# Attention and mixture of experts in one kernel: the first expert's weight casts ahead of the exponentials, six of their eight low parts on GpSimd

## The chip, the cores and the metric

The kernel runs on one core of a Trainium2 chip. The metric is the device time of one execution in microseconds; for the kernel before it is 588.51 us, the median of three runs (588.12 to 589.81).

## What is computed

```
attention, for 8 batches x 8 heads, 576 rows of 64:
    k_p, v_p = means of 8 neighbouring rows of k, v           # 72 rows each
    attn = softmax(q @ k_p.T / 8) @ v_p
x = attn as 4608 tokens of 512
experts, for each token:
    expert = argmax(x @ w_gate);  gate = softmax(x @ w_gate)[expert]
    out = gate * (relu(x @ w1[expert]) @ w2[expert])          # 512 -> 1024 -> 512, 8 experts
```

All tensors are float32. The expert products are made from a rounded part and a rest: a weight W is held as a "high part" (the weight rounded by a cast to the type fp32r) and a "low part" (the weight minus its high part), and a product is the sum of three matmuls.

## The kernel before, in words

The first 170 us or so of the 587.5 us span are attention. It runs as one hand-written loop over 36 tiles `t` of 128 tokens, in four groups `g` of nine. What a pass of the loop emits goes to each engine's queue in that order, and each engine takes its queue strictly in order. Per pass `t`, the steps are:

- `p_transpose(t)`: TensorE turns the exponentials `P` into `pP` (L314), ScalarE copies them to `pt` (L315, two copies).
- `scores(t+2)`: TensorE writes the scores into the one buffer `pS` (L288); VectorE takes their maximum `mx` (L294) and subtracts it into `sd` (L299). `sd` frees `pS` for the next pass's scores.
- `q_transpose(t+3)`: TensorE, then a ScalarE copy to `qT` (L280). In some passes there follow `v_expand` (L232, copy `V` L234: passes 25 to 28) or `kv_transpose` with four small copies (L212, L214: passes 20, 22 and 23).
- `weights(t+2)`: ScalarE's exponential of `sd` into `P` (L307); after it, in every third pass, a small exponential `ex` for the router (L382).
- `weigh(t)`: TensorE, `pt` times `V` into the one buffer `pU` (L330). A pass is counted below from one start of `weigh` to the next.
- `scale(t)`: VectorE divides (`r` L342, `lh` L344, `xe` L346); `xe` frees `pU`. Small steps of the router are woven in on VectorE: `rg`, `rm`, `rd`, `rk` at the end of each pass with `t % 3 == 2` (L412 to L416), `rn` and `ro` one pass later between `mx` and `sd` (L417, L377), then a count on TensorE and `rp`, `carry`, `rs` (L394, L395, L421). GpSimd multiplies `rp` by `ro` (L426), copies the token numbers (L422), casts a row index `ix` (L406) and issues the scatter of a tile's rows to DRAM (L449); VectorE makes the index as `rf` (L401, or L427 for the last batches).
- `w_split`: the last step of the passes 21 and 24 to 30. One eighth of the first expert's weights, loaded three passes earlier into one of four buffers (`w_load`, L460 on SyncE's queue), is cast on ScalarE (L466) and its low part is made by a subtraction (L467) with two inputs in SBUF, on VectorE, but on GpSimd in the passes 26 and 29.

"Cast 25" and "low part 25" mean those of pass 25 below, and `sd` 27 the `sd` of tile 27, which pass 25 makes. After the loop the tail of attention multiplies the first products with these weights, a plan is made, and the expert stage fills the rest of the span.

Of the kernel before, what the change touches and what calls it, by code (L numbers as in the profile page):

```python
# [15 lines left out]
ALU = mybir.AluOpType  # L16
# [17 lines left out]
NB = 3  # L34
# [6 lines left out]
W0T = (21, *range(24, 31))  # L41
# [12 lines left out]
def f32(a):  # L54
    return a.bitcast(F32)
# [48 lines left out]
def attention(ctx, outer, tc, q, k, v, wg, w1v, w2v, xs, W, cst, carry, tab, banks):  # L104
    nc = tc.nc
# [75 lines left out]
    def kv_load(g, i):  # L181


        src, c0 = (v if i % 2 else k), 3 * (i // 2)

        raw = u0["XE"][:, 0:3, :] if (g, i) == (0, 1) else kraw.tile([P, 3, 512], F32, tag="raw", name=f"raw{g}_{i}")
        sv = src[2 * g : 2 * g + 2].rearrange("b h (k8 x) d -> (b h k8) (x d)", k8=8)
        nc.sync.dma_start(out=raw, in_=sv[:, c0 * 512 : c0 * 512 + 1536].rearrange("p (c f) -> p c f", c=3))
        raws[g, i] = raw

    def kv_pool(g, i, eng):

        raw, c0, o = raws.pop((g, i)), 3 * (i // 2), 64 * (i % 2)

        def add(n):
            out = kvp[:, c0 : c0 + 3, o : o + 64] if n == 64 else raw[:, :, 0:n]
            return lambda: eng.tensor_tensor(out=out, in0=raw[:, :, 0:n], in1=raw[:, :, n : 2 * n], op=ALU.add)  # L197

        return [add(n) for n in (256, 128, 64)]
# [27 lines left out]
    def v_expand(g, i, bank, take=nc.scalar.copy):  # L227

        b, a = i // 2, i % 2
        for c in range(3 * a, 3 * a + 3):  # L230
            o, m, j = CH[c][0], CH[c][3], BL[c]
            nc.tensor.matmul(bank[0:R, j * 72 : (j + m) * 72], lhsT=vT[:, b * H * KP + o : b * H * KP + o + R],  # L232
                             rhs=wrhs[:, a, j : j + m].rearrange("p j f -> p (j f)"), start=True, stop=True)
        take(out=Vs[g % 2][0:R, b, a, :, 0 : D + NE], in_=bank[0:R, 0:360].rearrange("p (j f) -> p j f", f=D + NE))  # L234
# [9 lines left out]
    def q_load(g, b):  # L244
        t = e2.tile([P, 4, H, D], F32, tag="qa", name=f"qa{g}_{b}")
        src = q[2 * g + b, :, 0:512, :]
        if 2 * g + b < COPIED:

            t = t.rearrange("p x h d -> p (x h d)").rearrange("p (h x) -> p h x", h=H)
            nc.sync.dma_start(out=t, in_=src.rearrange("h (p x) d -> p h (x d)", x=4))  # L250
        else:
            for x in range(4):
                nc.sync.dma_start(out=t[:, x], in_=src.rearrange("h (p x) d -> x p h d", x=4)[x])
        qa[g, b] = t

    def qm_load(g):
        m = e1.tile([P, H, D], F32, tag="qm", name=f"qm{g}")
        for j in range(2):
            nc.sync.dma_start(out=m[64 * j : 64 * j + 64], in_=q[2 * g + j, :, 512:576, :].rearrange("h p d -> p h d"))
        qa[g, 2] = m  # L260
# [14 lines left out]
    def q_transpose(t):  # L275
        src = qr.pop(t).rearrange("p h d -> p (h d)")
        for j in range(4):
            nc.tensor.transpose(pq[:, j * P : (j + 1) * P], src[:, j * P : (j + 1) * P], ident)  # L278
        qT[t] = p3.tile([P, 512], F32, tag="qT", name=f"qT{t}")
        nc.scalar.copy(out=qT[t], in_=pq)  # L280

    def scores(t):
        g = t // NT
        for j in range(4):
            for p0, b in [(0, 0), (64, 1)] if KIND(t) == 4 else [(0, parts(t)[0][2]), (64, parts(t)[0][2])]:
                for hp in range(2):
                    r = slice(64 * hp, 64 * hp + 64)
                    nc.tensor.matmul(pS[p0 : p0 + 64, hp, j * SK : (j + 1) * SK], lhsT=qT[t][r, j * P + p0 : j * P + p0 + 64],  # L288
                                     rhs=kTs[g % 2][r, b, j, hp * SK : (hp + 1) * SK], start=True, stop=True, skip_group_check=True)
        for count, _ in counts:  # L290
            count()
        s4 = pS[:, :, 0:288].rearrange("p a (h x) -> p a h x", h=4)
        mx = p2.tile([P, 2, 4], F32, tag="mx", name=f"mx{t}")
        nc.vector.tensor_reduce(out=mx, in_=s4, axis=AX.X, op=ALU.max)  # L294
        if t - 2 in stores:
            stores.pop(t - 2)()
        weave()
        sd = p2.tile([P, 2, 4, SK], F32, tag="sd", name=f"sd{t}")
        nc.vector.tensor_tensor(out=sd, in0=s4, in1=mx.unsqueeze(3).to_broadcast([P, 2, 4, SK]), op=ALU.subtract)  # L299
        run(counted for _, counted in counts)  # L300
        counts.clear()
        weave(1, True)
        sds[t] = sd
# [5 lines left out]
    def p_transpose(t, take=nc.scalar.copy):  # L309
        pt[t] = [p2.tile([P, 3 * P], F32, tag=f"pt{a}", name=f"pt{a}_{t}") for a in range(2)]  # L310
        for a in range(2):
            for c in range(3):
                o = CH[3 * a + c][0]
                nc.tensor.transpose(pPs[a][0:R, c * P : (c + 1) * P], Ps[t % 2][:, o : o + R], ident)  # L314
            take(out=pt[t][a][0:R], in_=pPs[a][0:R, 0 : 3 * P])  # L315
# [141 lines left out]
    def w_load(i):  # L457

        raw = kraw.tile([P, 1024], F32, tag="raw", name=f"w0_{i}")
        nc.sync.dma_start(out=raw.rearrange("p (c f) -> p c f", c=4 if i < 4 else 2), in_=load_piece(w1v, w2v, 0, i))  # L460
        w0[i] = raw

    def w_split(i):
        raw = w0.pop(i)
        c, a = slice((i % 4) * 1024, (i % 4 + 1) * 1024), 0 if i < 4 else 2
        nc.scalar.copy(out=W[:, a, c], in_=raw)  # L466
        (nc.gpsimd if W0T[i] % NB == 2 else nc.vector).tensor_tensor(out=W[:, a + 1, c], in0=raw, in1=f32(W[:, a, c]), op=ALU.subtract)  # L467

# [44 lines left out]
    def run(fs):  # L515
        for f in fs:
            f()
# [67 lines left out]
    for t in range(total):  # L585
        g, i = divmod(t, NT)
        more = g + 1 < NG
        for (G, at), j in loads.items():
            if at == t:
                kv_load(G, j)  # L590
        if more:
            if i == 2:
                q_load(g + 1, 0)
            if i == 4:
                qm_load(g + 1)
            if i == 6:
                q_load(g + 1, 1)
        if t in first:
            run(kv_pool(*first.pop(t), nc.gpsimd))
        for at, n, *gj in adds:  # L600
            if at == t:
                third = tuple(gj)
                if third not in pieces:
                    pieces[third] = kv_pool(*gj, vec)
                halves.extend(pieces[third][:n])
                del pieces[third][:n]
        if t + 3 in W0T:
            w_load(W0T.index(t + 3))
        if 0 < t < total - 2:
            p_transpose(t)  # L610
        if 2 < t + 2 < total:
            scores(t + 2)
        counts.extend(picked)
        picked.clear()
        if t - 1 in pools:
            run(kv_pool(*pools.pop(t - 1), nc.gpsimd))
        if t + 3 < total:
            q_transpose(t + 3)
        elif t == total - 3:
            for s in (1, 2):  # L620
                x_split(s)()
        at = (2, 4, 5) if g else (3, 5, 6)
        if more and i in at:
            kv_transpose(g + 1, at.index(i), pm)
        if more and i >= 7:
            v_expand(g + 1, i - 7, pm)
        if i < 2:
            v_expand(g, 2 + i, pm)
        if t + 4 < total:
            q_copy(t + 4)  # L630
        if t + 2 < total:
            weights(t + 2)
        run(powers)
        powers.clear()
        if t == total - 3:
            p_transpose(t + 1)
        weigh(t)
        if t == total - 3:
            x_low = x_split(3)
            p_transpose(t + 2)  # L640
        if t == total - 4:
            x_split(0)()
        if t == total - 1:
            multiply(4)
        if t >= total - 3:
            weave(7)
        held = steps[:] if t == total - 1 else []
        if held:
            steps.clear()
        scale(t)  # L650
        if t == total - 3:
            x_low()
        for bt, (t0, nb) in enumerate(batches):
            if t == t0 + nb - 1:
                route(bt)
        if t in W0T:
            w_split(W0T.index(t))
        if 20 <= t < 24:
            clear_rows(t - 20)
        if t == total - 7:  # L660
            x_load()
        if t == total - 5:
            x_open()
            begun_load()
# [1107 lines left out]
```

## Time and profile before

| | |
|---|---|
| median of 3 runs | 588.51 us |
| profiled execution, its own time | 589.0 us |
| its span | 587.5 us |
| TensorE busy | 560.3 us (95%) |
| VectorE busy | 373.9 us (64%) |
| ScalarE busy | 244.8 us (42%) |
| GpSimd busy | 196.7 us (33%) |
[...]

The table's shares are averages over attention and experts. In the passes with a weight piece the picture is another: there TensorE stands still for part of each pass, and VectorE is the engine with the most work.

### The profile page before, as it was taken

To read this page: it belongs to the slowest core of one execution; us is meant where nothing else is said; L and a number is where in the kernel's file an instruction comes from. 1 tells how busy PE (TensorE), PEld (TensorE's weight loads), DVE (VectorE), ACT (ScalarE), POOL (GpSimd) and SP (SyncE) were. 2 spreads that over 40 slices of the span, in tenths; PEclk is the share of its full clock that TensorE was granted. 3 is DMA by queue.
4 is the path that set the end of the run, shared out by engine and by line. 5 is a ranking of instruction groups with operands and counts; after the bars stand their busy time and mean duration, and the time that the engine had idled before them with its cause. 6 is when DMAs were issued, how large, how long until landed. Compare 5 with 4: busy or idle time off the path is not lost.

```text
span 587.5 us, 13579 instructions
## 1 busy us (share of the span) xinstructions
PE 560.3 (95%) x4334; PEld 499.3 (85%) x4334; DVE 373.9 (64%) x749; ACT 244.8 (42%) x451; POOL 196.7 (33%) x293
## 2 busy tenths in 40 slices
PE   6899999998898999999999999999999999999994
PEld 5788989897787888879988889888899888888994
DVE  6699999988884224657949671685428956143221
ACT  2677676776631102357545420434115842021110
POOL 7456765625432042126232222151113451101101
PEclk9999999999999999999999999999999999999999
DMA  8969999994422647446996852046412750101001
GB/s 313 367 222 291 312 297 286 264 261 148 141 90 76 185 146 249 123 152 189 256 316 188 245 175 63 20 134 196 133 56 70 226 161 23 57 0 40 37 4 56
DMA packets 89013, 96.50 MB, mean 164 GB/s; under 512 B 38174, under 2 KB 69918, under 8 KB 88864
## 3 DMA queue, kind: packets, MB, share of 16 engines
q1 hardware_dynamic: 79472, 74.22, 43.3%
q0 software_dynamic: 8848, 20.55, 9.7%
q8 instruction: 60, 0.98, 0.7%
q14 instruction: 89, 0.73, 0.4%
q10 hardware_dynamic: 544, 0.02, 0.1%
HBM read 72.68 MB, written 26.00 MB: 168 GB/s over the span
## 4 chain that ended last, share of the span: by engine, by line
PE 76%; DVE 14%; issue 3%; DMA 3%; ACT 2%; POOLq 1%; DVEq 1%; SPq 0%; POOL 0%; ACTq 0%
PE pU L964 31%; PE pP L907 20%; PE pq L907 10%; PE pU L330 4%; DVE sd L299 2%; DVE mx L294 2%; PE pS L288 2%; DMA XE<-in_v_dram 2%; PE pP L314 2%; PE pP L506 2%; PE pq L278 1%; DVE xe L346 1%; DVE raw L197 1%; PE pm L232 1%; DVE W L467 1%
## 5 line engine op out<-in xcount | busy, mean ns | idle before, releaser
L964 PE MATMUL pU<-W,H 128*128 128x512 f32 x912 | 200.4, 380 | 2.5 <-issue 1.3
L964 PEld LDWEIGHTS pU<-W,H 128*128 128x128 f32 x912 | 171.6, 189 | 28.2 <-issue 2.7
L1595 POOL DMA_INDIRECT out_dram<-Y,GT x51 | 60.4, 1184 | 195.3 <-DVE Y L1389 164.6
L907 PE MATMUL pP<-X,W 128*128 128x512 f32 (+3 forms) x660 | 121.9, 340 | 2.0 <-DVEq L1645 1.5
L907 PEld LDWEIGHTS pP<-X,W 128*128 128x128 f32 x660 | 108.6, 190 | 11.9 <-DVEq L1645 1.9
L1099 ACT ACTIVATE H<-pP 128x512 fp32r<-128x512 f32 x56 | 33.5, 598 | 141.9 <-PE pP L907 135.5
L1389 DVE TENSOR_SCALAR Y<-pU,GT 128x512 f32<-128x512 f32 x36 | 26.8, 747 | 89.8 <-PE pU L964 89.8
L1120 DVE SCALAR_TENSOR_TENSOR H<-pP,H 128x512 fp32r<-128x512 f32 (+1 forms) x62 | 39.8, 643 | 57.1 <-ACT H L1099 54.9
L1205 ACT CAST W<-ST 128x1024 fp32r<-128x1024 f32 x56 | 56.8, 1050 | 23.9 <-PE pU L964 19.6
L1213 DVE TENSOR_TENSOR W<-ST,W 128x1024 fp32r<-128x1024 f32 x54 | 64.2, 1213 | 3.8 <-ACT W L1205 3.7
L907 PE MATMUL pq<-X,W 128*128 128x512 f32 (+3 forms) x324 | 62.4, 342 | 0.9 <-issue 0.9
L330 PE MATMUL pU<-V,pt 110*128 110x146 f32 (+3 forms) x468 | 56.9, 283 | 3.0 <-ACT pt L315 1.7
L907 PEld LDWEIGHTS pq<-X,W 128*128 128x128 f32 x324 | 53.8, 190 | 6.1 <-issue 1.3
L330 PEld LDWEIGHTS pU<-V,pt 110*128 110x128 f32 (+3 forms) x468 | 51.4, 179 | 5.4 <-ACT pt L315 3.8
L1602 POOL DMA_DIRECT2D GT<-dispatched x44 | 24.4, 554 | 83.3 <-issue 82.1
L1099 ACT ACTIVATE H<-pq 128x512 fp32r<-128x512 f32 x28 | 16.7, 598 | 60.3 <-PE pq L907 60.2
L449 POOL DMA_INDIRECT dispatched<-xe,ix x36 | 36.0, 1001 | 13.5 <-POOL ix L406 11.3
L1174 DVE STREAM_TRANSPOSE pS<-XE 128x512 f32<-128x512 f32 x26 | 37.7, 1492 | 0.0
L307 ACT ACTIVATE P<-sd 128x576 f32<-128x576 f32 x36 | 24.8, 688 | 24.4 <-DVE sd L299 19.1
L1120 DVE SCALAR_TENSOR_TENSOR H<-pq,H 128x512 fp32r<-128x512 f32 (+1 forms) x30 | 19.6, 654 | 23.7 <-ACT H L1099 23.1
L315 ACT COPY pt<-pP 110x384 f32<-110x384 f32 x72 | 30.8, 479 | 4.1 <-PE pP L314 3.5
L197 POOL TENSOR_TENSOR raw<-raw 128x768 f32<-128x768 f32 (+1 forms) x18 | 27.5, 1527 | 9.6 <-DMA raw<-in_v_dram 5.4
(213 smaller groups left out, 648.9 us busy)
## 6 DMA issues: line engine op xcount, KB each, us to landing
ST<-in_moe_w_dram SPq DMA_DIRECT2D x56, 512.0 KB, 5.8
raw<-in_k_dram SPq DMA_DIRECT2D x12, 768.0 KB, 7.8
raw<-in_v_dram SPq DMA_DIRECT2D x11, 768.0 KB, 9.2
XE<-dispatched SPq DMA_DIRECT2D x104, 64.0 KB, 4.0
qa<-in_q_dram SPq DMA_DIRECT2D x24, 256.0 KB, 6.8
w<-in_moe_w_dram SPq DMA_DIRECT2D x8, 512.0 KB, 6.8
XE<-dispatched SPq DMA_DIRECT2D x15, 256.0 KB, 4.4
qa<-in_q_dram SPq DMA_DIRECT2D x2, 1024.0 KB, 11.4
```

The costliest lines, as they stand in the source:

```text
L197: return lambda: eng.tensor_tensor(out=out, in0=raw[:, :, 0:n], in1=raw[:, :, n : 2 * n], op=ALU.add)
L315: take(out=pt[t][a][0:R], in_=pPs[a][0:R, 0 : 3 * P])
L330: nc.tensor.matmul(pu[p0 : p0 + n, a, h * VW : (h + m) * VW], lhsT=pt[t][a][0:r, c % 3 * P + p0 : c % 3 * P + p0 + n], rhs=Vs[g % 2][0:r, ...
L449: apart(nc.gpsimd.indirect_dma_start(out=xs, out_offset=bass.IndirectOffsetOnAxis(ap=at, axis=0), in_=rows, in_offset=None))
L907: r = pe.matmul(out=pH[g % 3][:, :m], lhsT=w1s(w, f, k), rhs=x, start=i == 0, stop=i == len(passes) - 1)
L964: r = pe.matmul(out=pY[:, s % 2, :], lhsT=h, rhs=in_turn(w[:, k * 512 : (k + 1) * 512]), start=start and i == 0, stop=stop and i == len(ps ...
L1099: act.activation(out=HH[:, f, o], in_=src[:, o], func=AF.Relu).then_inc(Q["A_h"], 1)
L1120: return dve.scalar_tensor_tensor(out=dst[:, f, to], in0=src[:, at], scalar=0.0, in1=f32(HH[:, f, at]), op0=ALU.max, op1=ALU.subtract)
L1174: dve.transpose(out=pX[:, s % 2, :].rearrange("p (c a g t) -> p c g t a", c=4, a=2, g=4), in_=XE[u % 2][:, s, :].rearrange("p (g r c) -> p ...
L1205: act.copy(out=(W1H if i < 4 else W2H)[:, o], in_=ST[:, i, :]).then_inc(Q["A_s1" if i < 4 else "A_s2"], 1)
L1213: eng.tensor_tensor(out=(W1L if i < 4 else W2L)[:, o], in0=ST[:, i, :], in1=f32((W1H if i < 4 else W2H)[:, o]), op=ALU.subtract).then_inc( ...
L1595: pool.indirect_dma_start(out=out, out_offset=bass.IndirectOffsetOnAxis(ap=GT[:, u, s, 1:2].bitcast(I32), axis=0), in_=Y[:, s, :], in_offs ...
```

## The change

In a pass with a weight piece the cast is emitted before `q_copy` and `weights(t+2)`, so it stands ahead of the exponential in ScalarE's queue. The low part stays at the end of the pass, but the engines are exchanged: GpSimd makes those of the passes 21, 24, 25, 27, 28 and 30, VectorE those of 26 and 29.

```
         nc.scalar.copy(out=W[:, a, c], in_=raw)
-        (nc.gpsimd if W0T[i] % NB == 2 else nc.vector).tensor_tensor(out=W[:, a + 1, c], in0=raw, in1=f32(W[:, a, c]), op=ALU.subtract)
+        return lambda: (nc.vector if W0T[i] % NB == 2 else nc.gpsimd).tensor_tensor(out=W[:, a + 1, c], in0=raw, in1=f32(W[:, a, c]), op=ALU.subtract)
...
             v_expand(g, 2 + i, pm)
+        if t in W0T:
+            w_low = w_split(W0T.index(t))
         if t + 4 < total:
             q_copy(t + 4)
...
         if t in W0T:
-            w_split(W0T.index(t))
+            w_low()
```

ScalarE, pass 28, as a difference (`w_5` is this pass's weight piece, `P` and `sd` belong to tile 30, `pt_29` to the next pass):

```order
 L280 COPY qT_2395<-pq 128x512
 L234 COPY V_147<-pm 110x5x72
+L466 CAST W<-w_5_2144 128x1024
 L307 ACTIVATE P_148<-sd_2382 128x2x4x72
-L466 CAST W<-w_5_2144 128x1024
 L315 COPY pt_29_2422<-pP_65 110x384
 L315 COPY pt_29_2423<-pP_66 110x384
```

The cast has moved from between the exponential and the copies of `pt` to ahead of the exponential.

GpSimd, the passes 28 to 31, before:

```order
L406 CAST ix_2277<-rf_2276 128x1
L449 DMA dispatched<-xe_2136,ix_2277 38400x514
L467 TENSOR_TENSOR W<-w_6_2212,W 128x1024
L426 TENSOR_TENSOR rp_2473<-rp_2473,ro_2472 128x24
L422 COPY xe_2339<-tok 128x3
```

and now:

```order
L406 CAST ix_2278<-rf_2277 128x1
L449 DMA dispatched<-xe_2137,ix_2278 38400x514
L467 TENSOR_TENSOR W<-w_5_2144,W 128x1024
L467 TENSOR_TENSOR W<-w_7_2284,W 128x1024
L426 TENSOR_TENSOR rp_2474<-rp_2474,ro_2473 128x24
L422 COPY xe_2340<-tok 128x3
```

Where one low part (29) stood behind the last of three scatters, two (28 and 30) now stand back to back, with nothing between them.

VectorE, the end of pass 29 and the beginning of pass 30, now:

```order
L414 TENSOR_TENSOR rd_2471<-rg_2470,rm_2475 128x24
L416 SCALAR_TENSOR_TENSOR rk_2472<-rd_2471,order 128x24
L467 TENSOR_TENSOR W<-w_6_2212,W 128x1024
L294 TENSOR_REDUCE mx_2528<-pS 128x8
L417 TENSOR_REDUCE rn_2476<-rk_2472 128x3
L377 TENSOR_TENSOR ro_2473<-rk_2472,rn_2476 128x24
L299 TENSOR_TENSOR sd_2532<-pS,mx_2528 128x576
```

Low part 29 now stands between `rk` and `mx`; before, `mx` followed `rk` directly.

## Rows read from the trace of the kernel before

**Rows 1.** Busy us per pass (start:end, length, each engine; clock, DMA, GB/s), passes 23–31.
```profile
117.92:121.27 3.35, 3.35 (x56) 3.09 (x55) 2.48 (x9) 3.17 (x8) 1.21 (x2) 1.00 1.08 296
121.27:125.44 4.17, 4.17 (x67) 3.87 (x65) 3.23 (x11) 2.75 (x6) 1.15 (x2) 1.00 0.97 234
125.44:129.99 4.55, 4.20 (x61) 3.90 (x61) 4.11 (x12) 3.34 (x7) 1.54 (x4) 1.00 0.98 331
129.99:134.31 4.32, 4.24 (x63) 3.81 (x61) 4.18 (x12) 3.11 (x7) 1.56 (x3) 1.00 0.67 205
134.31:139.28 4.97, 4.46 (x65) 3.94 (x65) 4.01 (x9) 3.33 (x8) 3.13 (x3) 1.00 0.36 109
139.28:143.85 4.57, 3.69 (x55) 3.19 (x55) 4.19 (x15) 3.37 (x7) 1.94 (x6) 1.00 0.36 143
143.85:148.49 4.64, 3.65 (x54) 3.12 (x55) 4.47 (x11) 2.72 (x6) 3.57 (x6) 1.00 0.39 144
148.49:153.46 4.97, 3.78 (x59) 3.25 (x59) 4.01 (x8) 2.98 (x7) 2.01 (x1) 1.00 0.47 110
153.46:157.33 3.87, 3.43 (x66) 2.89 (x67) 3.73 (x12) 2.09 (x5) 0.55 (x3) 1.00 0.56 168
```
The engines stand in the order TensorE, its weight loads, VectorE, ScalarE, GpSimd.

**Rows 2.** Timeline (start us, us, engine, line; idle before), passes 25 to 26.
```profile
128.41 1.03 ACT L466 CAST W<-w 128x1024 fp32r<-128x1024 f32 x1
...
129.48 1.23 DVE L467 TENSOR_TENSOR W<-w,W 128x1024 fp32r<-128x1024 f32 x1 [0.41 <-ACT W L466]
...
130.62 0.75 DVE L294 TENSOR_REDUCE mx<-pS 128x8 f32<-128x576 f32 x1
...
131.40 0.76 DVE L299 TENSOR_TENSOR sd<-pS,mx 128x576 f32<-128x576 f32 x1
...
132.25 0.69 ACT L307 ACTIVATE P<-sd 128x576 f32<-128x576 f32 x1 [1.21 <-DVE sd L299]
```
**Rows 3.** Timeline of VectorE and GpSimd around low part 26.
```profile
133.95 0.75 DVE L294 TENSOR_REDUCE mx<-pS 128x8 f32<-128x576 f32 x1
133.96 2.35 POOL L467 TENSOR_TENSOR W<-w,W 128x1024 fp32r<-128x1024 f32 x1 [0.97 <-ACT W L466]
...
134.89 1.47 DVE L377 TENSOR_TENSOR ro<-rk,rn 128x24 bf16<-128x24 f32 x1
```
**Rows 4.** Timeline: VectorE and GpSimd, both with operands in SBUF, earlier passes.
```profile
45.00 0.98 DVE L197 TENSOR_TENSOR raw<-raw 128x768 f32<-128x768 f32 x1
45.11 0.92 POOL L422 COPY xe<-tok 128x3 int32<-128x3 int32 x1
...
58.07 2.90 POOL L197 TENSOR_TENSOR raw<-raw 128x768 f32<-128x768 f32 x2
60.06 1.73 DVE L197 TENSOR_TENSOR raw<-raw 128x768 f32<-128x768 f32 x1
```
**Rows 5.** Timeline: GpSimd and VectorE at the end of pass 21.
```profile
111.08 0.98 POOL L449 DMA_INDIRECT dispatched<-xe,ix  x1 [0.28 <-POOL ix L406]
...
112.88 0.35 DVE L197 TENSOR_TENSOR kvp<-raw 128x192 f32<-128x192 f32 x1
...
114.46 0.75 DVE L294 TENSOR_REDUCE mx<-pS 128x8 f32<-128x576 f32 x1
```
**Rows 6.** Timeline: `mx` behind pass 23's router steps; then passes 28 and 29.
```profile
121.46 0.75 DVE L294 TENSOR_REDUCE mx<-pS 128x8 f32<-128x576 f32 x1
...
140.91 0.18 POOL L406 CAST ix<-rf 128x1 int32<-128x1 f32 x1 [3.20 <-DVE rf L401]
...
143.02 0.68 DVE L346 TENSOR_TENSOR xe<-pU,r 128x512 f32<-128x512 f32 x1
...
146.65 0.98 POOL L449 DMA_INDIRECT dispatched<-xe,ix  x1 [0.28 <-POOL ix L406]
...
148.14 2.35 POOL L467 TENSOR_TENSOR W<-w,W 128x1024 fp32r<-128x1024 f32 x1 [0.51 <-ACT W L466]
```
**Rows 7.** The weight pieces' tile: their loads, from issue to landing.
```profile
DMA to landing us min/median/max: 3.9/6.8/10.0
```

More of the change, by code (lines that the diff above doesn't have):

```diff
@@ L466, in w_split @@
         nc.scalar.copy(out=W[:, a, c], in_=raw)
-        (nc.gpsimd if W0T[i] % NB == 2 else nc.vector).tensor_tensor(out=W[:, a + 1, c], in0=raw, in1=f32(W[:, a, c]), op=ALU.subtract)
+        return lambda: (nc.vector if W0T[i] % NB == 2 else nc.gpsimd).tensor_tensor(out=W[:, a + 1, c], in0=raw, in1=f32(W[:, a, c]), op=ALU.subtract)
     def clear_rows(s):
@@ L628, in attention @@
             v_expand(g, 2 + i, pm)
+        if t in W0T:
+            w_low = w_split(W0T.index(t))
         if t + 4 < total:
@@ L656, in attention @@
         if t in W0T:
-            w_split(W0T.index(t))
+            w_low()
         if 20 <= t < 24:
```

## The prediction

> **What bounds the kernel now.** I read the page first, then cut the attention loop into its passes, then followed the order of work through single passes. Over the span TensorE is nearly always busy, and a change on ScalarE, VectorE and GpSimd can win only where TensorE stands still. Pass by pass one sees where that is [rows 1]: pass 23, without a weight piece, lasts 3.35 us and TensorE is busy for all of it; pass 24, which has `v_expand` and the router's count on top, lasts 4.17, again all busy. The passes 25 to 31 last 4.55, 4.32, 4.97, 4.57, 4.64, 4.97 and 3.87, together 31.89, and TensorE is short of work by 0.1 to 1.2 in each. [...]
>
> What closes the pass there is a ring over two engines [rows 2]. The cast starts at 128.41, behind the exponential; the low part waits 0.41 for it and takes 1.23; `mx` stands behind the low part in VectorE's queue (130.62), then `sd` (131.40), and the next exponential, for which ScalarE has idled 1.21, starts at 132.25. From 128.41 to the next cast that is exponential 0.69, cast 1.03, low part 1.23, `mx` 0.75 and `sd` 0.76 less small overlaps, some 4.4 us, against 3.35 to 4.17 of TensorE's work. In two passes a second thing is seen [rows 3, 6]: low part 26 runs on GpSimd from 133.96 to 136.31, and VectorE's `ro`, 24 elements a row, takes 1.47 and ends with it; the same happens beside low part 29, from 148.14 to 150.49.
>
> **What the change takes out.** The cast moves into the 1.21 us that ScalarE idles ahead of the exponential [rows 2]. At 1.03 it fits; it costs nothing as long as `sd` isn't ready earlier than the cast ends. Where it does, ScalarE's work in a pass with `v_expand` is about 3.3 us [rows 1], below TensorE's 4.1, so ScalarE doesn't become the bound. The low part leaves VectorE in six passes (1.14 from its start to the next instruction's, 130.62 less 129.48) and comes onto it in two. With both gone from the ring, TensorE's own work is next in line.
>
> **What it adds.** GpSimd's low part takes 2.35 [rows 3, 6] and nobody needs its result before the first products after the loop. What it costs comes from the port. Two rows show that GpSimd and a VectorE instruction whose operands both lie in SBUF exclude each other [rows 4]: VectorE's addition at 60.06 takes 1.73 beside GpSimd's (0.98 at 45.00), and GpSimd's copy at 45.11, three elements, takes 0.92 until VectorE's addition is over. `mx`, which reads PSUM, keeps its 0.75 beside a low part [rows 3]. So I need only look where `kvp`, `rd`, `rk`, `ro` or a low part on VectorE meets a low part on GpSimd.
>
> *Pass 21.* Cast 21 now ends about 111.3, GpSimd is free at 112.06 when its scatter is issued, and low part 21 runs to 114.41. `kvp` (two SBUF inputs), which started at 112.88, now waits until then and ends about 114.65; `mx` follows at about 114.58 where it stood at 114.46 [rows 5]. What VectorE saves by giving up the low part it pays here: a loss of 0.12.
>
> *Passes 22 to 24.* No further change: 23 and 24 are full already. All starts below are those of before plus 0.12: `weigh` 25 at 125.56.
>
> *Passes 25 and 26.* Both have `v_expand`, without the count; I take TensorE's own 4.1 (4.17 less a little over 0.1 for the count, with an estimate of 0.05 for the remaining stalls). Gains 0.45 and 0.22. `weigh` 27 at 133.76.
>
> *Pass 27.* Before, `ro` was held for 1.47 instead of about 0.18 by low part 26 [rows 3]. That stall goes, 1.29. But low part 26 is now on VectorE, just ahead of `mx`, 1.14 more. That leaves 0.15. Cast 27 no longer stands between the exponential and the copies of `pt` that `weigh` 28 needs; of the 0.51 that TensorE stood in this pass [rows 1] I give it half, an estimate. Gain 0.4; `weigh` 28 at 138.3.
>
> *Pass 28.* GpSimd is now late. VectorE reaches low part 26 3.54 after `weigh` 26 starts (as `mx` at 121.46 followed 117.92 [rows 1, 6]), at 133.2, and `mx` at 134.34. GpSimd's index and scatter follow `mx` (about 0.85 for it and `rf`, 0.24 for the cast, 0.28 and 0.98 for the scatter), so low part 27 runs from 136.7 to 139.05. Behind it stand the next cast of an index, its scatter and `rp`, for which VectorE's `xe` of this pass waits: before, it started 2.11 after that cast (143.02 less 140.91 [rows 6]), now at 141.15. `weigh` 29 followed `xe` by 0.83 (143.85 less 143.02 [rows 1, 6]): 142.0. So the pass lasts 3.7 instead of 4.57, a gain of 0.87; without GpSimd's lateness it would be 3.35.
>
> *Pass 29.* Nothing but TensorE's 3.35: gain 1.29, `weigh` 30 at 145.35.
>
> *Pass 30.* Here the change pays back. VectorE comes to low part 29 at 142.0 + 3.54 = 145.54. GpSimd comes to low part 28 when its three scatters are issued: before, the last ended at 147.63, which is 4.61 after `xe`, now 145.76. VectorE is ahead by 0.2, so it has the port until 146.77, and low part 28 runs from there to 149.12. `mx` follows low part 29 at 146.68 and `ro` 0.94 later (134.89 less 133.95 [rows 3]), at 147.6; it is held until 149.12. Low part 30 is waiting on GpSimd by then. I let `ro` go first, because VectorE's addition at 45.00 got in between GpSimd's instruction and the copy that was queued directly behind it [rows 4]. Before, `weigh` 31 started 2.97 after the low part that held `ro` ended (153.46 less 150.49), with cast 30 in it; without the cast (1.03 [rows 2], of which some 0.95 after overlaps) 2.0 remain: 151.15. The pass lasts 5.8 instead of 4.97: a loss of 0.83.
>
> *Pass 31.* No low part ahead of `mx`: 3.35 instead of 3.87, gain 0.52.
>
> The sum: -0.12 + 0.45 + 0.22 + 0.4 + 0.87 + 1.29 - 0.83 + 0.52 = 2.8 us. What follows (the last passes, the plan, the experts) hangs on this chain and I let it move along whole. The profiled execution took 589.0 (span 587.5, 1.5 around it), which becomes 586.2; it lay 0.5 above the median, so against 588.51 the forecast is **585.7 us**.
>
> **What else is queued behind the moved steps.** On SyncE a weight load waits for the low part that frees its buffer. Low part 24 would end at about 126.2, low part 25 at 130.6, low part 26 at 134.4; the loads behind them are needed by the casts 28, 29 and 30, at about 139, 142 and 146. That leaves some 11.7 us, and the loads take 3.9 to 10.0 [rows 7]. A later load would now hold the exponential behind the cast, us for us. The three scatters of pass 28 are issued earlier than before (145.76 against 147.63), so the token load that waits for them isn't late. Both cost nothing; for the first the cover is 1.7 us.
>
> **The rivals.** *GpSimd wins one of the two races in pass 30.* If low part 30 gets the port ahead of `ro`, `ro` is held to 151.47 and pass 30 ends at 153.5: 2.35 of the gain is gone, 588.1. If low part 28 starts ahead of low part 29, VectorE waits to 148.13, subtracts to 149.3, and `ro` then meets low part 30, until 151.65: 588.2. For it: the race is lost by 0.2 only, a difference of sums with ten terms. Against it: both queues hang on the same `xe`, so the common terms cancel.
>
> *No collision in pass 30.* If low part 28 is done before `ro` comes, or an instruction as small as `ro` isn't held, it ends at about 147.8, `weigh` 31 starts at 149.8, and 1.35 more is gained: 584.4. Against it stand 1.47 in the trace [rows 3] and three scatters in GpSimd's queue.
>
> *VectorE loses what it gives away.* If a low part on GpSimd holds VectorE's queue whatever stands in it, each of the six costs VectorE at least the 1.14 that it spares, and the time stays at 588.5. For it: `kvp` and `ro`. Against it: `mx` kept its 0.75 beside a low part [rows 3], and `sd`, `lh` and `xe` read PSUM as it does. [...]
>
> *Slower: both low parts ahead of VectorE's.* Low part 28 gets the port first and low part 30, whose cast is done by 147.2, keeps it, so VectorE's low part 29 stands from 145.54 until 150.48, `mx` and `sd` behind it and TensorE's scores behind `sd`. `mx` starts at 151.63, `sd` some 1.1 later, `weigh` 31 at about 154.8: 3.6 later than forecast, 589.3. It decides from the point at which GpSimd is first by any margin and keeps the port over an instruction boundary. A load that lands more than 11.7 us after issue would add to it.
>
> **How the numbers follow.** Chances: forecast 0.52, GpSimd wins one race 0.23, no collision 0.10, VectorE loses what it gives 0.05, slower 0.10. A difference below 0.3% (1.8 us) can't be told from none, so faster means below 586.7, slower above 590.3. Of the forecast, whose terms I trust to about 1 us together, 0.45 lies below 586.7 and 0.07 above; with the case without a collision and 0.01 of the others faster gets 0.56. The slower case lies mostly inside 0.3%; with late loads on top 0.07 lie beyond. Same is 0.37. The range goes from 584.2, the case without a collision, to 588.7, both cases in which a race is lost; about 0.2 lies outside.
>
> **What would show it right or wrong.** ScalarE's casts in the passes 25 to 30 ahead of the exponentials, and the idle time before those gone; `kvp` of pass 21 at about 1.8 us instead of 0.35; the passes 25, 26 and 29 at 4.1, 4.1 and 3.35; `xe` of pass 28 waiting for GpSimd; a long low part 28 (3.3 us, 1.0 of it waiting) and `ro` of pass 30 held for 1.5 us. A short `ro`, or pass 30 below 5 us, would mean the no-collision case; a `ro` of 3.5 us or a low part 29 of more than 3 us one of the lost races. If `mx` or `sd` are longer than 0.76 beside low parts, my reading of the port is wrong, and if the gain by pass 32 isn't found at the end, what follows isn't hanging on this chain.

## The result, and the profile after

The changed kernel is slower: 596.22 us median (593.49 to 597.80, 6 runs) against 589.16 for the kernel before in the same runs, a ratio of 1.0112 with the 95% interval 1.0076 to 1.0147. The forecast of 585.7 us, and its range up to 588.7, missed on the wrong side.

| profiled execution | before | after |
|---|---|---|
| time | 589.0 us | 595.5 us |
| span | 587.5 us | 594.0 us |
| passes 21 to 31 together | 48.12 us | 53.50 us |
| VectorE busy | 373.9 us | 376.0 us |
| GpSimd busy | 196.7 us | 205.1 us |
| mean granted TensorE clock | 0.998 | 0.989 |

The eleven passes with the weight pieces hold 5.38 of the 6.5 us. Another 1.0 lies ahead of pass 21, where both kernels issue the same work (`weigh` 21 starts at 110.22 instead of 109.21; in the profiled executions of the experiments it lay between 109.48 and 112.08). What moves it isn't shown. From `weigh` 32 to the end it is 430.2 us before and 430.3 after.

Busy us per pass of the kernel after, cut as in [rows 1] (start:end, length, TensorE, its weight loads, VectorE, ScalarE, GpSimd; clock, DMA share, GB/s); passes 21 and 22, then 25 to 31:

```profile
110.22:116.96 6.74, 4.01 (x64) 3.51 (x62) 6.60 (x13) 4.94 (x11) 4.09 (x4) 0.99 1.08 316
116.96:122.17 5.21, 5.21 (x70) 4.57 (x70) 3.69 (x13) 1.68 (x4) 1.55 (x4) 0.68 0.77 230
...
129.62:133.70 4.08, 4.08 (x63) 3.83 (x62) 3.12 (x11) 3.36 (x7) 3.77 (x6) 1.00 0.90 260
133.70:137.70 4.00, 4.00 (x62) 3.75 (x61) 2.72 (x9) 3.29 (x7) 1.98 (x3) 1.00 0.68 217
137.70:142.24 4.54, 4.25 (x68) 3.96 (x67) 4.30 (x12) 3.53 (x8) 2.68 (x3) 1.00 0.78 222
142.24:145.70 3.46, 3.46 (x56) 3.05 (x55) 2.63 (x12) 2.83 (x6) 2.72 (x7) 1.00 0.30 119
145.70:149.13 3.43, 3.43 (x56) 3.17 (x56) 2.88 (x8) 2.88 (x5) 2.87 (x5) 1.00 0.39 150
149.13:159.61 10.48, 4.59 (x60) 3.90 (x59) 9.63 (x11) 3.08 (x6) 4.94 (x3) 0.75 0.47 129
159.61:163.72 4.11, 4.11 (x67) 3.62 (x67) 2.61 (x10) 2.13 (x4) 0.75 (x4) 0.80 0.02 4
```

Read the length against [rows 1]. The passes 25 to 29 take 19.51 us where they took 23.05, a gain of 3.54, and TensorE is busy in nearly all of it. Nearly everything is lost in two places: passes 21 and 22 (6.74 and 5.21 instead of 4.50 and 4.21) and pass 30 (10.48 instead of 4.97); pass 31 adds 0.24. In pass 30 VectorE reads as busy for 9.63 us with 11 instructions. That is the sign to look for: few instructions, much time.

Timeline around pass 21 of the kernel after (start us, us, engine, line, operation; idle before):

```profile
111.07 1.05 ACT L466 CAST W<-w 128x1024 fp32r<-128x1024 f32 x1
...
112.06 0.96 POOL L449 DMA_INDIRECT dispatched<-xe,ix  x1 [0.28 <-POOL ix L406]
...
112.42 3.41 DVE L197 TENSOR_TENSOR raw<-raw 128x384 f32<-128x384 f32 x1
...
112.54 0.69 ACT L307 ACTIVATE P<-sd 128x576 f32<-128x576 f32 x1 [0.41 <-DVE sd L299]
...
113.06 2.35 POOL L467 TENSOR_TENSOR W<-w,W 128x1024 fp32r<-128x1024 f32 x1
...
116.72 0.35 DVE L197 TENSOR_TENSOR kvp<-raw 128x192 f32<-128x192 f32 x1
...
116.96 0.51 PE L330 MATMUL pU<-V,pt 110*64 110x146 f32 x2 [2.56 <-DVE xe L346]
```

Scatter and low part stand where [rows 5] and the forecast let one expect them, 1.0 later with the pass, and `kvp` comes only after the low part and keeps its 0.35. But `raw` takes 3.41. This `raw` (L197) is VectorE's addition of 128x384, one of those that form the means of k and v, of which `kvp` is the last. Before, it took 0.55, inside the scatter of [rows 5]:

```profile
111.44 0.55 DVE L197 TENSOR_TENSOR raw<-raw 128x384 f32<-128x384 f32 x1
```

In the kernel after, it starts 0.64 us ahead of the recorded start of low part 21 and ends 0.42 behind its end (115.83 against 115.41). `xe` stands behind it in VectorE's queue, and `weigh` 22 waits for `xe` for 2.56 us.

Timeline around pass 30 of the kernel after, the same columns:

```profile
148.44 0.98 POOL L449 DMA_INDIRECT dispatched<-xe,ix  x1 [0.28 <-POOL ix L406]
...
148.99 5.16 DVE L414 TENSOR_TENSOR rd<-rg,rm 128x24 f32<-128x24 f32 x1
...
149.45 4.65 POOL L467 TENSOR_TENSOR W<-w,W 128x1024 fp32r<-128x1024 f32 x2
...
154.29 1.22 DVE L467 TENSOR_TENSOR W<-w,W 128x1024 fp32r<-128x1024 f32 x1
...
155.42 0.75 DVE L294 TENSOR_REDUCE mx<-pS 128x8 f32<-128x576 f32 x1
...
156.39 0.75 DVE L299 TENSOR_TENSOR sd<-pS,mx 128x576 f32<-128x576 f32 x1
...
157.24 0.69 ACT L307 ACTIVATE P<-sd 128x576 f32<-128x576 f32 x1 [6.38 <-DVE sd L299]
...
157.29 1.24 PE L288 MATMUL pS<-kT,qT 64*64 64x72 f32 x32 [5.89 <-DVE r L342]
```

`rd`, 24 elements a row, starts 0.46 us ahead of the recorded start of low part 28 and stands until both low parts, 28 and 30, are over (154.15 and 154.10). The low parts run back to back (4.65 us for the two), and `rd` doesn't get in between them. Behind `rd` wait low part 29, `mx` and `sd`; behind `sd` the exponential, for 6.38 us, and TensorE, for 5.89.

### The profile page after: what moved, and what is told of

Its sections match the earlier page's. It is cut to its first block, busy times and chain, and to the rows that moved or that the text cites. A ratio compares the mean times of both kernels' runs of the same rounds, so it can differ in the third digit from the quotient of the medians.

```text
span 594.0 us, 13580 instructions
## 1 busy us (share of the span) xinstructions
PE 564.2 (95%) x4334; PEld 502.2 (85%) x4334; DVE 376.0 (63%) x745; ACT 244.9 (41%) x451; POOL 205.1 (35%) x297
## 4 chain that ended last, share of the span: by engine, by line
PE 80%; DVE 10%; DMA 3%; issue 3%; SPq 1%; ACT 1%; DVEq 1%; POOL 0%; POOLq 0%; ACTq 0%
PE pU L966 31%; PE pP L909 18%; PE pq L909 10%; PE pU L330 6%; PE pS L288 3%; PE pP L314 2%; PE pq L278 2%; DMA XE<-in_v_dram 2%; PE pP L506 2%; DVE raw L197 2%; PE pm L232 1%; DVE mx L294 1%; DVE sd L299 1%; DVE xe L346 1%; DVE rd L414 1%
## 5 line engine op out<-in xcount | busy, mean ns | idle before, releaser
L330 PE MATMUL pU<-V,pt 110*128 110x146 f32 (+3 forms) x468 | 58.6, 294 | 3.7 <-DVE xe L346 3.0
L330 PEld LDWEIGHTS pU<-V,pt 110*128 110x128 f32 (+3 forms) x468 | 53.2, 188 | 5.6 <-ACT vT L214 2.8
L288 PE MATMUL pS<-kT,qT 64*64 64x72 f32 x1152 | 26.8, 232 | 7.2 <-DVE r L342 6.2
L288 PEld LDWEIGHTS pS<-kT,qT 64*64 64x64 f32 x1152 | 21.6, 135 | 13.8 <-issue 12.5
```

Of the source, the lines that this page charges most:

```text
L330: nc.tensor.matmul(pu[p0 : p0 + n, a, h * VW : (h + m) * VW], lhsT=pt[t][a][0:r, c % 3 * P + p0 : c % 3 * P + p0 + n], rhs=Vs[g % 2][0:r, ...
```

## The experiments

"The port" is the prediction's name for what a low part on GpSimd and a VectorE instruction with two SBUF inputs don't have at the same time; the runs show when each of the two starts and ends, not what lies behind it. The theory ("port from issue" in the expectations): a low part on GpSimd has the port while the scatter ahead of it on GpSimd is still being made, so well ahead of its recorded start, and low parts that follow one another keep it. Every VectorE instruction with two SBUF inputs that comes after that stands until the last is over. Two rivals: GpSimd has the port only from the recorded start (and `raw` and `rd` are long for another reason), and the cast ahead of the exponential is what costs. In the 3.41 and 5.16 above, instructions with two SBUF inputs stood until the low parts were over. From when a queued low part holds them is what the experiments are about. None of the kernels leaves out any part of the computation.

**The casts alone.** The low parts stay on the engines of the kernel before.

```
-        return lambda: (nc.vector if W0T[i] % NB == 2 else nc.gpsimd).tensor_tensor(...)
+        return lambda: (nc.gpsimd if W0T[i] in (26, 29) else nc.vector).tensor_tensor(...)
```

> Only the order on ScalarE is changed: the casts ahead of the exponentials, the low parts on the engines of before (GpSimd in the passes 26 and 29). Theory, port from issue: the loss of the changed kernel sits in the passes 21 and 30, where a low part on GpSimd holds VectorE; here pass 21 is as before (raw 0.55, kvp 0.35) and at most one low part (29) stands behind the scatters, so no instruction of VectorE is held for more than about 2.8 us. The cast leaves the ring, the low part doesn't: 0.3 to 0.6 us less in each of the passes 25 to 28, together 1 to 3 us faster than before. Rival, the cast: the exponentials come too late behind the casts; then this kernel is slower than before by most of the 7 us.

Measured: 588.46 us, ratio 0.9979 (0.9961 to 0.9996); the passes 21 to 31 together 45.58. The casts ahead are a gain of 2.5 us in these passes, and the rival that they cost falls. (In the profiled execution pass 21 starts 2.9 us later than before, so its span, 588.0, doesn't show the gain; the median is 1.3 us lower.) One meeting is left, in pass 30 (timeline):

```profile
148.24 2.36 POOL L467 TENSOR_TENSOR W<-w,W 128x1024 fp32r<-128x1024 f32 x1
148.40 2.25 DVE L414 TENSOR_TENSOR rd<-rg,rm 128x24 f32<-128x24 f32 x1
```

`rd` ends at 150.65, low part 29 at 150.60. Pass 30 takes 5.77.

**The engines alone.** The casts stay behind the exponentials.

```
-        if t in W0T:
+        if t in W0T and t not in (21, 24, 25, 26, 27, 28, 29, 30):
             w_low = w_split(W0T.index(t))
...
+        if t in (21, 24, 25, 26, 27, 28, 29, 30):
+            w_low = w_split(W0T.index(t))
         if t in W0T:
             w_low()
```

> Only the engines of the low parts are exchanged; the casts stay behind the exponentials. Theory, port from issue: cast 21 ends after raw and kvp of pass 21 have begun, so low part 21 is issued too late to hold raw, and pass 21 is near 4 us instead of 6.74; low part 30 can't follow low part 28 directly, since its cast waits for an exponential that waits for the held VectorE, so the hold in pass 30 is one low part long (up to 2.9 us), not two. The passes 25 to 29 gain less than in the changed kernel, because the cast stands ahead of the copies of pt. Together within 2 us of before. Rival, the engines alone: if exchanging the engines is what costs, whatever the order, this kernel is as slow as the changed one, 5 us or more over before.

Measured: 591.41 us, ratio 1.0031 (1.0015 to 1.0047); passes 21 to 31 50.47. With the late cast, low part 21 isn't recorded before 114.69; `raw` (112.76) keeps its 0.55 and pass 21 is 4.53. In pass 30 low part 28 holds `rd` alone, because cast 30, and with it low part 30 (154.82), comes later:

```profile
146.50 0.99 POOL L449 DMA_INDIRECT dispatched<-xe,ix  x1 [0.28 <-POOL ix L406]
...
147.05 2.88 DVE L414 TENSOR_TENSOR rd<-rg,rm 128x24 f32<-128x24 f32 x1
147.52 2.36 POOL L467 TENSOR_TENSOR W<-w,W 128x1024 fp32r<-128x1024 f32 x1
```

Again `rd` starts inside the scatter, 0.47 ahead of the low part's recorded start, and is held. So each half of the change is needed for the whole loss: the early cast puts low part 21 in front of `raw` and low part 30 right behind 28.

**Low part 28 without 30.** Low parts 21 and 30 go back to VectorE (24, 25, 27 and 28 stay on GpSimd).

> The changed kernel with the low parts 21 and 30 on VectorE (GpSimd: 24, 25, 27, 28). Theory, port from issue: pass 21 as before (about 4.4 us, raw 0.55), and in pass 29 rd is held to the end of low part 28 alone, 2.4 to 2.9 us instead of 5.16; pass 30 about 7 us instead of 10.48, the total about 5 us below the changed kernel and within 2 us of before. Rival, port from the recorded start: rd starts ahead of the recorded start of low part 28 and so isn't held; low part 29 or ro waits instead, and the total is about 586.

Measured: 589.98 us, ratio 1.0001 (0.9981 to 1.0020); passes 21 to 31 47.66. `rd` took 2.88 (145.70 to 148.58) beside one low part (146.16, 2.37), against 5.16 beside two. The second low part costs its own 2.3 us to `rd`, which doesn't get in at the boundary between the two.

**A probe.** The changed kernel with a small addition of two SBUF tiles on VectorE behind `sd` in the passes 23 (where GpSimd has a scatter and no low part) and 27 (scatter, then low part 27).

```
+        if t in (25, 29):
+            nc.vector.tensor_tensor(out=probe[:, 0:8], in0=cst["order"], in1=cst["capv"], op=ALU.add)
```

> The changed kernel with one more small VectorE instruction (8 elements a row, both inputs in SBUF, result unused) behind sd in the passes 23 and 27. In pass 23 no low part stands behind the scatter; in pass 27 low part 27 does, its cast done, and its recorded start is 0.6 us after the probe's. Theory, port from issue: about 0.18 us in pass 23 and about 3 us in pass 27, ending when low part 27 ends. Rival, port from the recorded start: 0.18 us in both.

Timeline of VectorE and GpSimd in pass 23, then in pass 27 (the inserted lines move line numbers by 3, so L302 is the probe, L452 the scatter and L470 the low part):

```profile
123.99 1.02 POOL L452 DMA_INDIRECT dispatched<-xe,ix  x1 [0.28 <-POOL ix L409]
124.11 0.16 DVE L302 TENSOR_TENSOR probe<-order,capv 128x8 f32<-128x8 f32 x1
...
141.49 0.96 POOL L452 DMA_INDIRECT dispatched<-xe,ix  x1 [0.28 <-POOL ix L409]
141.85 3.02 DVE L302 TENSOR_TENSOR probe<-order,capv 128x8 f32<-128x8 f32 x1
142.48 2.35 POOL L470 TENSOR_TENSOR W<-w,W 128x1024 fp32r<-128x1024 f32 x1
```

The same instruction takes 0.16 beside a scatter alone and 3.02 beside a scatter with a low part queued behind it, from 0.63 ahead of the low part's recorded start until 0.04 behind its end. So it isn't the scatter that holds the probe. At its 0.16 it would have been over 0.47 us ahead of the recorded start (141.85 + 0.16 against 142.48), so it was held from a point at least that far ahead; for `rd` in the kernel after the same sum gives 0.28. The rival of the recorded start falls here. (The time, 597.43 us, is of one run.)

The early hold was seen only for a low part that stood ready behind a scatter. In the kernel before, low part 26 had to wait for its cast (133.96, [rows 3]), and `rk`, which started 0.11 ahead of it with two SBUF inputs, kept its 0.18:

```profile
133.85 0.18 DVE L416 SCALAR_TENSOR_TENSOR rk<-rd,order 128x24 f32<-128x24 f32 x1
```

The probe's run also has one meeting that VectorE won: low part 29 (155.89) took its usual 1.22, and low part 30 on GpSimd, which had waited for its cast until 156.13, was recorded 3.17 long instead of 2.35. So GpSimd didn't go first in this meeting, and the 0.82 us that low part 30 took longer stand inside its recorded duration.

**No meeting.** Only 24, 25 and 27 stay on GpSimd, behind which nothing with two SBUF inputs comes in time.

```
-        return lambda: (nc.vector if W0T[i] % NB == 2 else nc.gpsimd).tensor_tensor(...)
+        return lambda: (nc.gpsimd if W0T[i] in (24, 25, 27) else nc.vector).tensor_tensor(...)
```

> The changed kernel with the low parts 21, 28, 29 and 30 on VectorE, so that GpSimd makes only 24, 25 and 27: the three behind which no VectorE instruction with two SBUF inputs came within their time. Theory (all of the loss comes from the meetings at raw of pass 21 and rd of pass 30, and from the clock that fell behind them): raw 0.55, rd 0.17, pass 21 about 4.1 us, pass 22 4.4, pass 29 3.5 to 3.8, pass 30 about 4.4, pass 31 about 3.7 and the clock 1.00 in all; passes 21 to 31 together 43.6 to 44.0 instead of 53.5 (before: 48.1). The time is 4 us below the kernel before, ratio 0.992 to 0.994. Rival (a pass that costs TensorE's neighbours more than the meetings, so that the loss moves elsewhere): the sum stays above 46 and the ratio above 0.997.

**No meeting, low part 21 late.** The same with 21 on GpSimd and its cast alone behind the exponential.

> As the run with only 24, 25 and 27 on GpSimd, but low part 21 is on GpSimd too and its cast stays behind the exponential, as in the kernel before. With the engines exchanged alone that low part was recorded from 114.69, after raw (112.76) was over. Theory (what decides is when the low part is issued, not that it is on GpSimd): raw 0.55, kvp short too, pass 21 about 4.5 and pass 22 about 3.7, together 8.2 instead of 8.5; passes 21 to 31 43.3 to 43.7, ratio 0.992 to 0.994. Rival (a low part 21 on GpSimd holds VectorE in any position): pass 21 above 5.5.

**All on VectorE.** GpSimd makes no low part.

> The changed kernel with all eight low parts on VectorE; GpSimd makes none, and the casts stay ahead of the exponentials. It asks what the move to GpSimd is worth by itself. Theory (the cast in the ring was what cost, the low parts on VectorE fit beside TensorE's work once the cast is out of it): no instruction of VectorE is held, passes 26 to 29 4.0, 4.5, 3.7 and 3.8, pass 30 4.4; passes 21 to 31 43.7 to 44.3, within 0.4 us of the run with three on GpSimd. Rival (VectorE is the bound in the passes 25 to 31, as the prediction had it, so each low part that comes back costs up to 1.14): 24, 25 and 27 on VectorE cost 1 to 3 us against that run.

**Two low parts later.** GpSimd makes 28 and 30 behind the scatters of pass 31.

```
         if t in W0T:
-            w_low()
+        if t in W0T and t not in (28, 30):
+            w_low()
+        if t == 28:
+            w_late = w_low
+        if t == 31:
+            w_late()
+            w_low()
```

> GpSimd makes 24, 25, 27, 28 and 30, VectorE 21, 26 and 29; but the low parts 28 and 30 are put on GpSimd behind the scatters of pass 31 instead of behind the passes 28 and 30. Theory (GpSimd's low parts cost only where they meet): passes 28 to 31 about 3.5, 3.5, 4.4 and 3.5, with the clock at 1.00, since rd of pass 30 finds the port free. The two low parts are then issued about 7 us after weigh 31, and the next rd, some 11 us after it, falls into the second of them: held about 1 us in pass 33, of which TensorE, with the last tiles, feels a part. Passes 21 to 31 43.0 to 43.8, ratio 0.992 to 0.995. Rival (the loss hangs on what GpSimd does and not on the meeting): passes 30 or 31 stay above 5.5.

These four ran side by side (before: 591.32 us there, 35 runs; 589.73 us, 25 runs, beside the first four). Their medians are 589.59, 588.84, 589.42 and 593.26 us. Pass lengths of the profiled executions in us, from `weigh` to `weigh`:

| kernel | 21 | 22 | 25 to 29 | 30 | 31 | 21 to 31 | 33 | ratio to before |
|---|---|---|---|---|---|---|---|---|
| before | 4.50 | 4.21 | 23.05 | 4.97 | 3.87 | 48.12 | 3.14 | 1 |
| after | 6.74 | 5.21 | 19.51 | 10.48 | 4.11 | 53.50 | 3.14 | 1.0112 |
| casts alone | 4.05 | 4.40 | 20.23 | 5.77 | 3.67 | 45.58 | 3.15 | 0.9979 |
| engines alone | 4.53 | 3.68 | 20.97 | 7.95 | 5.81 | 50.47 | 3.15 | 1.0031 |
| 28 without 30 | 4.13 | 4.40 | 19.53 | 7.33 | 4.82 | 47.66 | 3.15 | 1.0001 |
| no meeting | 4.06 | 7.34 | 19.90 | 4.84 | 3.66 | 48.24 | 4.44 | 0.9976 (0.9956 to 0.9995) |
| no meeting, 21 late | 4.56 | 5.30 | 19.91 | 4.83 | 3.67 | 45.72 | 5.84 | 0.9965 (0.9950 to 0.9979) |
| all on VectorE | 4.22 | 4.39 | 20.19 | 4.84 | 3.66 | 44.75 | 4.98 | 0.9970 (0.9944 to 0.9996) |
| two later | 4.19 | 4.75 | 19.53 | 4.53 | 3.36 | 43.82 | 7.59 | 1.0031 (1.0009 to 1.0054) |

For the passes 21 and 30 the theory held. Without a meeting pass 21 is at 4.06 to 4.22 and pass 30 at 4.53 to 4.84; low part 21 on GpSimd holds nothing when it comes after `raw` (`raw` 0.55, pass 21 4.56 against 4.50 before). For the sums and the times my expectations failed: the sum of 48.24 and the ratio of 0.9976 of the kernel with no meeting are what its rival had named, a loss that moves elsewhere. In the last kernel the two low parts hold the next `rd`, as far as they overlap it:

```profile
161.81 4.67 POOL L467 TENSOR_TENSOR W<-w,W 128x1024 fp32r<-128x1024 f32 x2
...
163.61 2.91 DVE L414 TENSOR_TENSOR rd<-rg,rm 128x24 f32<-128x24 f32 x1
```

`rd` ends at 166.52, the low parts at 166.48. I had expected a hold of 1 us there; the whole kernel became slower.

The kernel without any low part on GpSimd takes 28.69 us for the passes 25 to 31 (20.19 + 4.84 + 3.66) and the one with three there 28.40. So once the casts are moved, the low parts on GpSimd, where they meet nothing, are worth 0.3 us. The 3.2 us between 31.89 and 28.69 are not of the casts alone, since that kernel also takes the low parts 26 and 29 back to VectorE: the casts alone have 29.67 there, a gain of 2.2, and the other 1.0 is mostly the meeting in pass 30 (5.77 against 4.84). Nor do the two halves of the change add up. In the passes 25 to 29 the casts alone gain 2.82 us, the engines alone 2.08 and both together 3.54: either breaks most of the ring of [rows 2]. All these are pass lengths of one profiled execution each.

What I had wrong is how much of this reaches the end: the times of the first three are 0.24 to 0.35% below before, where I had expected 0.6 to 0.8 for two of them. The profiled executions show three places where it is given back. Two of these executions lie 2.2 and 2.4 us above the medians of their kernels (591.05 with low part 21 late, 591.80 with all on VectorE), so how often it is given back isn't known.

First pass 22 (7.34 and 5.30). In both kernels TensorE stops inside the score products, 27 of 32 done, and the profile shows nothing that it waited for ("issue"). TensorE's timeline, the kernel with no meeting:

```profile
116.46 0.68 PE L288 MATMUL pS<-kT,qT 64*64 64x72 f32 x27 [0.64 <-DVE rs L421]
119.12 0.35 PE L288 MATMUL pS<-kT,qT 64*64 64x72 f32 x5 [1.98 <-issue]
```

and the one with low part 21 late:

```profile
117.12 0.71 PE L288 MATMUL pS<-kT,qT 64*64 64x72 f32 x27
119.13 0.35 PE L288 MATMUL pS<-kT,qT 64*64 64x72 f32 x5 [1.29 <-issue]
```

A packet of a DMA queue of the kind `instruction` begins at 116.8 and 116.5, 3.3 and 1.6 us behind `weigh` 22. In the kernels before, after, casts alone, engines alone, 28 without 30 and all on VectorE it begins 0.2 to 3.5 us ahead of `weigh` 22, and the 32 products run through in 0.73. In the kernel with two later it begins 1.2 us behind, and the products take longer there too, with a pause ahead of the same 28th product:

```profile
117.98 1.09 PE L288 MATMUL pS<-kT,qT 64*64 64x72 f32 x32 [0.65 <-DVE rs L421]
```

In all three the 28th product starts 1.2 to 1.4 us after the packet has ended (117.91, 117.82 and 117.33; the products 119.12, 119.13 and 118.72). So the late packet goes with the stop; that it is the cause was not tried.

Second, pass 33. In all four kernels of this set `mx` and ScalarE's copy of the transposed rows to `X` start late. Timeline, the kernel with all on VectorE:

```profile
160.47 0.76 DVE L294 TENSOR_REDUCE mx<-pS 128x8 f32<-128x576 f32 x1 [1.20 <-PE pP L314]
...
161.21 0.58 ACT L498 CAST X<-pq 128x512 fp32r<-128x512 f32 x1 [2.87 <-PE pP L314]
```

and the kernel before at the same place:

```profile
161.52 0.59 ACT L498 CAST X<-pq 128x512 fp32r<-128x512 f32 x1 [0.60 <-PE pq L496]
...
161.76 0.75 DVE L294 TENSOR_REDUCE mx<-pS 128x8 f32<-128x576 f32 x1
```

In the first the products that they read are done at 158.23 and 158.91, and the two engines idle for 1.20 and 2.87 us; before, neither waited like this. In these four kernels GpSimd's scatters of pass 32 wait 2.2 to 4.2 us for a load from the same table; with the casts alone it is 1.24, and in the four others without the probe they wait 0.83 and not for this load. Whether that or something else holds the two engines stays open; no run was made for it.

Third, the granted clock behind pass 33. Pass 33, pass 34 and what follows with all on VectorE, in the columns of [rows 1]:

```profile
159.88:164.86 4.98, 3.58 (x28) 3.31 (x27) 3.60 (x10) 3.53 (x7) 0.82 (x1) 0.86 0.27 102
164.86:167.80 2.94, 2.94 (x17) 2.94 (x15) 2.33 (x11) 0.60 (x2) 0.24 (x2) 0.50 0.00 0
167.80:172.00 4.20, 4.20 (x17) 3.81 (x16) 2.15 (x9) 0.22 (x1) 3.23 (x5) 0.50 0.33 125
```

and the passes 33 and 34 with no meeting:

```profile
162.84:167.28 4.44, 3.05 (x29) 2.72 (x27) 3.60 (x10) 3.15 (x7) 0.87 (x1) 1.00 0.32 118
167.28:169.52 2.24, 1.69 (x17) 1.50 (x15) 1.83 (x11) 0.82 (x3) 0.18 (x1) 1.00 0.00 0
```

In both TensorE stood 1.4 us in pass 33, but only in the first did the clock fall, to 0.50. From `weigh` 34 to the end that kernel takes 425.3 us against 421.9 before, which is 3.4 us and more than pass 33 itself loses (1.8). With two later it is the same picture (0.50, 424.6 us). What decides whether the clock falls there stays open. Over the runs of the kernel with no meeting the time goes with the clock: the four runs with a mean clock of 0.997 or more took 587.1 to 588.5 us, the five with 0.991 or less 590.0 to 592.0.

The lowest median is that of no meeting with low part 21 late: 588.84 against 591.32 before, 2.5 us. Its interval overlaps those of no meeting, of all on VectorE and of the casts alone, so which of the four is best can't be told.

## Why the prediction was wrong

**Passes 25 to 29: right.** Forecast were 4.1, 4.1, 4.57, 3.7 and 3.35, together 19.82; measured 4.08, 4.00, 4.54, 3.46 and 3.43, together 19.51. In the ring of [rows 2] the cast now stands in ScalarE's idle time, the exponential follows without idling, and VectorE waits for TensorE's scores instead of the other way round (timeline, pass 25):

```profile
130.17 1.05 ACT L466 CAST W<-w 128x1024 fp32r<-128x1024 f32 x1
...
131.12 0.69 ACT L307 ACTIVATE P<-sd 128x576 f32<-128x576 f32 x1
...
132.18 2.35 POOL L467 TENSOR_TENSOR W<-w,W 128x1024 fp32r<-128x1024 f32 x1
...
132.66 0.76 DVE L294 TENSOR_REDUCE mx<-pS 128x8 f32<-128x576 f32 x1 [0.28 <-PE pS L288]
...
133.45 0.76 DVE L299 TENSOR_TENSOR sd<-pS,mx 128x576 f32<-128x576 f32 x1
```

`mx` and `sd` keep 0.76 beside a low part, so the rival that VectorE loses what it gives away falls, and the reading by operands (these two read `pS` in PSUM) held here. The weight loads are in time: they land 5.0 to 9.2 us after issue, and no cast waits for one. VectorE was not the engine with the most work in all of these passes before: by [rows 1] it was in 28 to 31 (4.19 against TensorE's 3.69 in pass 28), while in 24 to 27 it was TensorE (4.46 against 4.01 in pass 27). And the split of the gain was not right: I needed both halves for it, the cast and the low part, and the runs show that either alone gives most of it here (2.82 and 2.08 of 3.54).

**Pass 21: the step that failed.** "`kvp` ..., which started at 112.88, now waits until then": it did not, `kvp` took 0.35. Low part 21 came when I had it (113.06, with the pass 1.0 later; forecast 112.06). What was wrong is that I let it hold VectorE only from there. `raw`, which started 0.64 us ahead of it, was not even on my list, because before it was over (111.99) when the scatter of [rows 5] was (112.06). A loss of 0.12 was forecast, 2.24 was measured.

**Pass 22: a term left out.** "No further change" for the passes 22 to 24. TensorE had stood for 2.56 us, and the next pass ran with a granted clock of 0.68, busy all the time: 5.21 instead of 4.21 (with the engines alone, also busy all the time but at 1.00, it took 3.68). In the passes of [rows 1] TensorE was short of work by at most 1.2 us each, and the clock stayed at 1.00.

**Pass 30: the step that decided.** "VectorE is ahead by 0.2, so it has the port until 146.77." By recorded starts this came out well: `rd` started at 148.99 and takes 0.18 unhindered, so `rk` and low part 29 (0.10 behind the start of `rk`) would have begun near 149.2 and 149.3, and low part 28 is recorded from 149.45. But the recorded starts didn't decide it here. `rd`, two instructions ahead of low part 29, was held although it started 0.46 ahead of the recorded start of low part 28. "I let `ro` go first" failed as well: nothing of VectorE's got in at the boundary between GpSimd's two low parts (`rd` stood 5.16), and the row that I took it from (a VectorE addition that got in, [rows 4]) was no guide to it; why it got in there isn't shown. Forecast were 5.8 us, measured 10.48. The pass with one low part instead of two (7.33) and with none that meets (4.84) price the two halves: 2.5 for the first, 3.2 for the second with the lower clock.

**The slower rival** had the order that was measured, GpSimd first and nothing of VectorE's between its two low parts, with a chance of 0.10 and 589.3 us. It was too small in three terms: it held VectorE from low part 29 on, not from `rd` (pass 30 would have been 9.4), it had no second place (pass 21), and no clock.

**Pass 31.** Forecast 3.35, measured 4.11 with TensorE busy all the time at a granted clock of 0.80, in the pass behind the 5.89 us without work.

**The tail.** That what follows moves along whole held for this change (430.2 and 430.3). It did not hold for the last four experiments, whose pass 33 grew by 1.3 to 4.5 us, with up to 3.4 us more behind it.

With the measured terms in place of mine the sum is 48.12 + 2.24 + 1.00 - 0.07 (pass 24) - 3.54 + 5.51 + 0.24 = 53.50.

## What to carry to other kernels

Before work like these low parts is moved to GpSimd, list every VectorE instruction with two SBUF inputs that can start shortly ahead of the GpSimd instruction's recorded start (here 0.46 to 0.64 us) or beside it, above all when the GpSimd instruction stands ready behind a scatter. A tiny instruction on the critical path (`rd`, 0.18 us unhindered) paid the whole length of the big one here (2.88), and two big ones in a row counted as one (5.16). Where a cast or copy can be moved into idle time of its own engine, test that part alone first: here it held 2.82 of the 3.54 us gained in the passes 25 to 29, and lost 0.8 in pass 30 (5.77 against 4.97).

## What the runs showed of the hardware that I had not expected

All of this is read from the traces of the runs that are named; it holds for these instructions, and what lies behind the holds and the clock isn't shown.

- VectorE instructions with two SBUF inputs were held to the end of a low part on GpSimd that stood ready behind a scatter, although they began 0.46 to 0.64 us ahead of its recorded start: `raw` 3.41 instead of 0.55 and `rd` 5.16 instead of 0.18 (the kernel after), `rd` 2.88 (the engines alone, and 28 without 30), the probe 3.02 instead of 0.16. By their unhindered lengths they would have been over 0.47 us ahead of that start (the probe) and 0.28 (`rd` in the kernel after). Beside a scatter alone the probe took 0.16, and in the kernel before a low part that waited for its cast didn't hold `rk`, which began 0.11 ahead (0.18).
- `rd` stood 2.88 us beside one low part (28 without 30) and 5.16 beside two back to back (the kernel after): it didn't get in between them.
- In the kernel after, the granted clock was 0.68 in pass 22, after TensorE had stood 2.56 us, and 0.75 and 0.80 in the passes 30 and 31, with 5.89 us without work in pass 30; with no meeting it was 0.77 in pass 23, after 1.98 us in pass 22. After 1.29 us (no meeting, low part 21 late, pass 22) it stayed at 1.00; after 1.40 in pass 33 it fell to 0.50 in one run (all on VectorE) and after 1.39 stayed at 1.00 in another (no meeting). Pass 22 of the kernel after, at 0.68, added 1.0 us to the 2.24 lost in pass 21.
- In two runs TensorE stood 2.0 us (no meeting) and 1.3 us (low part 21 late) in the middle of a row of products, where a packet of a DMA queue of the kind `instruction` had begun 3.3 and 1.6 us behind `weigh` 22; in a third (two later), where it began 1.2 us behind, the same row took 1.09 us instead of 0.73. No run here shows more than that they go together.
